# Joining small groups of matmuls in a fused attention and SwiGLU kernel: key products behind a batch's last totals, the turning of values and sums in front of the first query products

One Trainium2 chip (trn2), one core. The metric is the time of one execution on the device in microseconds (us); lower is better.

## The reference

```python
# q, k, v: (4, 4, 1088, 32) fp32; S1, S2: (8, 32)
def phi(x):                                   # features: 8 x 8 products of two sketches
    a = np.einsum('rd,bhsd->bhsr', S1, x)
    b = np.einsum('rd,bhsd->bhsr', S2, x)
    return np.einsum('bhsi,bhsj->bhsij', a, b).reshape(*x.shape[:-1], 64)
q_p, k_p = phi(q), phi(k)
kv = np.einsum('bhsf,bhsd->bhfd', k_p, v)     # "values"
z = np.sum(k_p, axis=2)                       # "sums"
num = np.einsum('bhsf,bhfd->bhsd', q_p, kv)   # "totals": numerator ...
den = np.einsum('bhsf,bhf->bhs', q_p, z)[..., None] + 1e-06    # ... and denominator
attn = num / den
x = attn.transpose(0, 2, 1, 3).reshape(4352, 128)
# feed-forward: w_gate, w_val (128, 1536), w_out (1536, 128)
g = x @ w_gate
out = (g / (1 + np.exp(-g)) * (x @ w_val)) @ w_out
```

## The kernel before

Each of the four batches is three blocks of up to 384 rows of x; a block has 12 "units" (a gate and a value matmul, silu on ScalarE, a product on VectorE that gives `hj`) and 12 down products, which accumulate in one PSUM bank, `acc`. After a block's last down product, VectorE transposes `acc` into the output tile ("store transpose"). The attention of batch b + 1 is a generator, stepped between the units of batch b. The parts that the change touches:

```python
def attention(b):
    for c0, c1 in kpieces:                 # two pieces: 5 and 4 chunks of keys
        turn_k(c0, c1)                     # DVE transpose of the loaded keys
        if c1 == NC and b + 1 < B:
            load_k(b + 1)
        yield
    phk = ...
    prods = [key_products(wide(t)[:, 0, :], *c) for t, c in zip("ab", kpieces)]
    key_features(phk, prods[0], *kpieces[0])
    yield
    key_features(phk, prods[1], *kpieces[1])
    zs = feature_sums(phk)                 # GpSimd
    yield
    kvp = wide("a")
    key_values(kvp[:, 0, :], phk, 0, NC)
    ...                                    # sums, copy to kvs, load_v, turn_q
    yield
    kzp = wide("b")[:, 0, 0 : 2 * P]...
    for t in range(2):
        turn_kv(kvs[:, t, :], kzp[:, t, :])     # "turning" of values and sums
    nc.scalar.copy(kvz[:], kzp)
    yield
    tags = "ab"
    for i, (x0, n) in enumerate(steps):
        phq = query_features(n, query_products(x0, n, tags))
        ...                                # turn_q of the next step, or load_q
        yield
        divide(b, x0, n, totals(n, phq, kvz, side_by_side(tags[0])))
        tags = tags[::-1]
        yield

def down():
    i, j = todo.pop(0)
    if j == 0:
        acc[i] = bank("g0" if i == 1 else "acc")
    nc.tensor.matmul(acc[i][:, 0:n], wo[:, j, :], hidden[i, j][:, 0:n], ...)
    if j == NCH - 1:
        store(i, n)                        # DVE transpose of acc, then DMAs

# (cut) end of the first batch:
while todo:
    for _ in range(3):
        if todo: down()
    next(att, None)
groups = (0, 1, 3, 4, 8, 11, 14, 17, 20, 23, 26, 29)    # units behind which attention steps
for b in range(1, B):
    att = attention(b + 1) if b + 1 < B else None
    for z in range(3 * NCH):
        unit(...)
        for _ in range(2):
            if len(todo) > LAG: down()     # LAG = 2
        if att and z in groups: next(att)
```

`wide("a")` and `wide("b")` are pairs of PSUM banks. The gate and value banks rotate over three banks once the down products have begun.

## Time and profile before

| | before |
|---|---|
| time, median (runs) | 322.25 us (322.06 to 322.41) |
| span of the profiled run | 319.9 us |
| TensorE (PE) busy | 312.2 us, 98% |
| VectorE (DVE), ScalarE (ACT), GpSimd (POOL) busy | 49%, 31%, 12% |
| first key product of the attention passes starts | 59.44 us |
| from there to the start of the last matmul: "the stream" | 256.07 us |

A row of the timeline is its start, its length, the engine, the line and the tiles; an fp32 matmul is two rows. Lengths overlap on PE, so the differences between starts are what is read.

### The profile page before, as it was taken

How to read it: one execution, taken by the hardware profiler on the slowest of the kernel's cores; microseconds unless marked ns; L12 is line 12 of the kernel's file. 1: busy time of each engine (PE TensorE's matmuls, PEld its weight loads, DVE VectorE, ACT ScalarE, POOL GpSimd, SP SyncE). 2: the span in 40 equal slices, each digit the busy share in tenths (PEclk: the TensorE clock that was granted, in tenths of full speed). 3: DMA queues.
4: the chain of work that ended last, by engine and by line, in shares of the span. 5: the costliest groups of instructions: out<-in, count | busy, mean ns of one | idle time of the engine just before them, and what ended most of it. 6: DMA issues, size and time to landing. Idle time of an engine off the chain costs nothing.

```text
span 319.9 us, 5604 instructions
## 1 busy us (share of the span) xinstructions
PE 312.2 (98%) x2300; PEld 193.7 (61%) x2300; DVE 157.8 (49%) x332; ACT 99.0 (31%) x227; POOL 37.6 (12%) x53
## 2 busy tenths in 40 slices
PE   8989999999999999999999999999999999999994
PEld 6545565655556665555666656555667655676664
DVE  4887999442556532554643542354544332323321
ACT  3467755321211322222322222313222222222230
POOL 2324234072000230000000060000000000000000
PEclk9999999999999999999999999999999999999999
DMA  7553490204041201100210100100010100100101
GB/s 206 155 151 100 162 243 2 72 0 97 2 94 27 65 22 50 27 0 2 39 58 0 22 2 0 24 4 2 0 27 0 21 0 2 26 0 0 21 2 25
DMA packets 24665, 13.99 MB, mean 44 GB/s; under 512 B 18368, under 2 KB 22720, under 8 KB 24640
## 3 DMA queue, kind: packets, MB, share of 16 engines
q1 hardware_dynamic: 24000, 13.54, 16.7%
q8 instruction: 18, 0.29, 0.4%
q10 hardware_dynamic: 640, 0.10, 0.2%
q14 instruction: 7, 0.06, 0.1%
HBM read 11.41 MB, written 2.23 MB: 43 GB/s over the span
## 4 chain that ended last, share of the span: by engine, by line
PE 88%; DVE 7%; issue 2%; ACT 1%; POOL 0%; DVEq 0%
PE bank L519 49%; PE bank L547 27%; DVE hj L533 2%; PE a L351 2%; PE a L401 2%; PE b L351 1%; PE bank L197 1%; PE a L307 1%; DVE exp L227 1%; PE a L561 1%; DVE man L231 1%; PE b L401 1%; PE a L276 1%; DVE exp L219 1%; ACT exp L224 1%
## 5 line engine op out<-in xcount | busy, mean ns | idle before, releaser
L533 DVE TENSOR_TENSOR hj<-sg,bank 128x384 f32<-128x384 f32 (+1 forms) x138 | 72.7, 528 | 118.2 <-PE bank L519 117.3
L525 ACT ACTIVATE sg<-bank 128x384 f32<-128x384 f32 (+1 forms) x144 | 67.9, 472 | 162.7 <-PE bank L519 161.9
L519 PE MATMUL bank<-xT,wg 128*128 128x384 f32 (+1 forms) x288 | 113.7, 477 | 1.2 <-POOL wg L235 1.1
L519 PE MATMUL bank<-xT,wv 128*128 128x384 f32 (+1 forms) x288 | 111.5, 469 | 0.5 <-DVE hj L533 0.5
L547 PE MATMUL bank<-hj,wo 128*128 128x384 f32 (+2 forms) x288 | 106.8, 462 | 0.3 <-DVE hj L533 0.2
L519 PEld LDWEIGHTS bank<-xT,wv 128*128 128x128 f32 x288 | 54.4, 190 | 34.5 <-DVE hj L533 2.1
L547 PEld LDWEIGHTS bank<-hj,wo 128*128 128x128 f32 x288 | 53.9, 190 | 33.2 <-issue 2.4
L519 PEld LDWEIGHTS bank<-xT,wg 128*128 128x128 f32 x288 | 52.7, 190 | 32.3 <-issue 3.9
L453 POOL TENSOR_TENSOR zs<-phk 128x1024 f32<-128x1024 f32 x3 | 7.0, 2348 | 115.5 <-PE bank L519 106.0
L379 DVE TENSOR_TENSOR phq<-a,qb 128x384 f32<-128x384 f32 (+1 forms) x11 | 5.8, 531 | 10.7 <-ACT qb L365 10.7
L365 ACT COPY qb<-a 128x384 f32<-128x384 f32 (+1 forms) x11 | 5.1, 460 | 15.1 <-PE b L351 8.6
L351 PE MATMUL a<-qT,sq 32*64 32x192 f32 (+1 forms) x176 | 9.2, 324 | 0.0
L351 PE MATMUL b<-qT,sq 32*64 32x192 f32 (+1 forms) x176 | 9.2, 324 | 0.0
L227 DVE SCALAR_TENSOR_TENSOR exp<-raw,exp 128x384 int32<-128x384 int32 (+2 forms) x14 | 8.6, 618 | 0.9 <-ACT exp L224 0.9
L224 ACT ACTIVATE exp<-exp,rebias 128x384 int32<-128x384 int32 (+3 forms) x15 | 8.2, 550 | 2.7 <-DVE exp L219 2.0
L422 DVE STREAM_TRANSPOSE dT<-a 128x384 f32<-128x384 f32 (+1 forms) x8 | 4.4, 550 | 7.8 <-PE a L401 7.8
L365 ACT COPY qb<-b 128x384 f32<-128x384 f32 (+1 forms) x11 | 5.1, 463 | 9.7 <-PE b L351 6.4
L575 DVE STREAM_TRANSPOSE o<-bank 128x384 f32<-128x384 f32 (+2 forms) x12 | 6.6, 549 | 2.7 <-PE bank L547 2.3
L351 PEld LDWEIGHTS a<-qT,sq 32*64 32x64 f32 x176 | 5.5, 131 | 3.9 <-issue 3.0
L379 DVE TENSOR_TENSOR phq<-b,qb 128x384 f32<-128x384 f32 (+1 forms) x11 | 5.8, 527 | 4.2 <-ACT qb L365 4.2
L231 DVE SCALAR_TENSOR_TENSOR man<-raw,man 128x384 f32<-128x384 uint32 (+2 forms) x14 | 6.9, 493 | 0.0
L225 ACT ACTIVATE man<-man 128x384 f32<-128x384 int32 (+3 forms) x15 | 6.7, 450 | 0.5 <-DVE man L220 0.5
(96 smaller groups left out, 168.9 us busy)
## 6 DMA issues: line engine op xcount, KB each, us to landing
kld<-in_k_dram SPq DMA_DIRECT2D x4, 544.0 KB, 4.1
vld<-in_v_dram SPq DMA_DIRECT2D x12, 144.0 KB, 4.3
qld<-in_q_dram SPq DMA_DIRECT2D x3, 544.0 KB, 3.9
raw<-in_moe_w_out_dram SPq DMA_DIRECT2D x4, 384.0 KB, 5.8
out_dram<-o SPq DMA_DIRECT2D x28, 48.0 KB, 1.9
raw<-in_moe_w_gate_dram SPq DMA_DIRECT2D x3, 384.0 KB, 3.3
raw<-in_moe_w_val_dram SPq DMA_DIRECT2D x3, 384.0 KB, 3.5
out_dram<-o SPq DMA_DIRECT2D x16, 40.0 KB, 1.7
```

The lines of the kernel that those rows point to most:

```text
L224: nc.scalar.activation(e[:], e[:], AF.Relu, bias=rebias[: shape[0], :], scale=8.0)
L227: nc.vector.scalar_tensor_tensor(out=e[:], in0=hi, scalar=-(1 << 31), in1=e[:], op0=ALU.bitwise_and, op1=ALU.bitwise_or,)
L231: nc.vector.scalar_tensor_tensor(out=f, in0=lo, scalar=2.0**-52, in1=f, op0=ALU.mult, op1=ALU.add)
L351: nc.tensor.matmul(parts[g][F * half : F * half + F, t, 0:w], sq[r, t, :, :].rearrange("p i j -> p (i j)"), qT[r, x0 : x0 + n, half, :], s ...
L365: nc.scalar.copy(qb[:, :, 0:w], both[:, :, 1, 0:w])
L379: nc.vector.tensor_tensor(out=phq[:, 2 * pr : 2 * pr + 2, 0:w], in0=both[:, :, 0, 0:w], in1=qb[:, :, 0:w], op=ALU.mult,)
L401: nc.tensor.matmul(halves(nd[t])[half][32 * h : 32 * h + 32, 0:w], kvz[t][r, 32 * h : 32 * h + 32], phq[r, h, 0:w], start=True, stop=True,)
L453: add = lambda o, a, b: nc.gpsimd.tensor_tensor(out=o, in0=a, in1=b, op=ALU.add)
L519: nc.tensor.matmul(o[:, 0:n], w[:, j, :], xT[:, t0 : t0 + n], start=True, stop=True)
L525: nc.scalar.activation(sg[:, 0:n], g[:, 0:n], AF.Silu)
L533: nc.vector.tensor_tensor(out=hj[:, 0:n], in0=sg[:, 0:n], in1=u[:, 0:n], op=ALU.mult)
L547: nc.tensor.matmul(acc[i][:, 0:n], wo[:, j, :], hidden[i, j][:, 0:n], start=(j == 0), stop=(j == NCH - 1),)
```

## The change

Its intent: fewer separate groups of small matmuls in the stream of large ones. The turning and the first query products become one step; the next batch's key products go directly behind the last totals, and their copies behind both of their parts. The key transposes therefore move ahead, and with fewer steps the units at which they stand move too. The diff, with three hunks cut (they split `key_products` into the products and `key_copy`, and call the two one after the other in the start-up):

```diff
@@ -457,15 +459,23 @@
         add(s[:, 0, :], s[:, 0, :], rows[:, 8, :])
         return s[:, 0, :].rearrange("p (h f) -> p h f", h=H)
 
-    def attention(b):
-
-        for c0, c1 in kpieces:
-            turn_k(c0, c1)
-            if c1 == NC and b + 1 < B:
-                load_k(b + 1)
-            yield
+    def next_keys(tag):
+
+        both = wide(tag)
+        for i, c in enumerate(kpieces):
+            key_products(both[:, i, :], *c)
+        return [key_copy(both[:, i, :], *c) for i, c in enumerate(kpieces)]
+
+    def attention(b, prods=None):
+
+
+        if prods is None:
+            for c in kpieces:
+                turn_k(*c)
+                yield
+            load_k(b + 1)
+            prods = next_keys("b")
         phk = apool.tile([P, NC, H, R, R], FP32, tag="phk", name="phk")
-        prods = [key_products(wide(t)[:, 0, :], *c) for t, c in zip("ab", kpieces)]
         key_features(phk, prods[0], *kpieces[0])
         yield
         key_features(phk, prods[1], *kpieces[1])
@@ -484,12 +494,11 @@
         turn_q(*steps[0])
         yield
         kvz = apool.tile([P, 2, P], FP32, tag="kvz", name="kvz", bufs=2)
-        kzp = wide("b")[:, 0, 0 : 2 * P].rearrange("p (t n) -> p t n", t=2)
+        kzp = bank()[:, 0 : 2 * P].rearrange("p (t n) -> p t n", t=2)
         for t in range(2):
             turn_kv(kvs[:, t, :], kzp[:, t, :])
         nc.scalar.copy(kvz[:], kzp)
         kvz = kvz[:, 0, :], kvz[:, 1, :]
-        yield
         tags = "ab"
         for i, (x0, n) in enumerate(steps):
             phq = query_features(n, query_products(x0, n, tags))
@@ -497,9 +506,20 @@
                 turn_q(*steps[i + 1])
             elif b + 1 < B:
                 load_q(b + 1)
+                turn_k(*kpieces[1])
+                if b + 2 < B:
+                    load_k(b + 2)
             yield
-            divide(b, x0, n, totals(n, phq, kvz, side_by_side(tags[0])))
+            nd = totals(n, phq, kvz, side_by_side(tags[0]))
+            last = i + 1 == len(steps)
+            if last and b + 1 < B:
+                prods = next_keys(tags[1])
+            divide(b, x0, n, nd)
+            if i == 1 and b + 1 < B:
+                turn_k(*kpieces[0])
             tags = tags[::-1]
+            if last:
+                return prods
             yield
 
 
@@ -736,28 +757,40 @@
         if z in groups:
             next(att)
     todo.sort()
+    keys = None
+
+    def attend():
+
+        nonlocal att, keys
+        try:
+            if att:
+                next(att)
+        except StopIteration as end:
+            att, keys = None, end.value
+
     while todo:
         for _ in range(3):
             if todo:
                 down()
-        next(att, None)
-    run(att)
-
-
-
-    groups = (0, 1, 3, 4, 8, 11, 14, 17, 20, 23, 26, 29)
+        attend()
+    while att:
+        attend()
+
+
+
+    groups = (0, 1, 6, 9, 12, 15, 18, 21, 24)
     for b in range(1, B):
-        att = attention(b + 1) if b + 1 < B else None
+        att = attention(b + 1, keys) if b + 1 < B else None
         for z in range(3 * NCH):
             i, j = z // NCH, z % NCH
             unit(3 * b + ((0, 2, 1)[i] if b == B - 1 else i), j)
             for _ in range(2):
                 if len(todo) > LAG:
                     down()
-            if att and z in groups:
-                next(att)
-        if att:
-            run(att)
+            if z in groups:
+                attend()
+        while att:
+            attend()
     ps = wide("a")[:, 0, 0:D]
     for j in range(NCH):
         if todo and j % 4 == 0:
```

More of the change, by code (lines that the diff above doesn't have):

```diff
@@ L269, in turn_q, with key_products @@
         )
-    def key_products(ps, c0, c1, aside=False):
+    def key_products(ps, c0, c1):
         for c in range(c0, c1):
@@ L282, in key_products, with key_copy @@
                 )
+    def key_copy(ps, c0, c1, aside=False):
         n = c1 - c0
@@ L620 @@
         turn_k(*c)
-    prods = [
-        key_products(bank(t), *c, aside=(c[1] == NC))
-        for t, c in zip(("g1", "g2", "acc"), fpieces)
-    ]
+    prods = []
+    for t, c in zip(("g1", "g2", "acc"), fpieces):
+        ps = bank(t)
+        key_products(ps, *c)
+        prods.append(key_copy(ps, *c, aside=(c[1] == NC)))
     phk = apool.tile([P, NC, H, R, R], FP32, tag="phk", name="phk")
```

## The prediction

> **What bounds the kernel now.** I read the page's busy table and its row of the granted clock, then the chain that ended last, then the waits by pair, and then the PE timeline around every group of small attention matmuls.
>
> ```profile
> PE 312.2 (98%) x2300; PEld 193.7 (61%) x2300; DVE 157.8 (49%) x332; ACT 99.0 (31%) x227; POOL 37.6 (12%) x53
> ...
> PEclk9999999999999999999999999999999999999999
> ...
> PE 88%; DVE 7%; issue 2%; ACT 1%; POOL 0%; DVEq 0%
> PE bank L519 49%; PE bank L547 27%; DVE hj L533 2%; PE a L351 2%; PE a L401 2%; PE b L351 1%; PE bank L197 1%; PE a L307 1%; DVE exp L227 1%; PE a L561 1%; DVE man L231 1%; PE b L401 1%; PE a L276 1%; DVE exp L219 1%; ACT exp L224 1%
> ```
>
> TensorE is busy in 98% of the span at a full clock and makes up 88% of the chain: a change pays only if it shortens the PE stream, or fills a hole in it. 76% of the chain is the feed-forward matmuls (L519 gate and value, L547 down), which the change does not touch. Busy does not mean free of overhead, because a matmul's row covers its latency as well, so I went by start times. A 384-column fp32 matmul is two rows; in the timeline such pairs start 0.645 us apart, a 320-column pair 0.54 us. Now the key products of the second batch, and the values and sums being turned:
>
> ```profile
> 104.60 0.81 PE L547 MATMUL bank<-hj,wo 128*128 128x384 f32 x2
> 105.34 0.80 PE L276 MATMUL a<-s,kT 128*64 128x64 f32 x20
> 105.97 0.64 PE L276 MATMUL b<-s,kT 128*64 128x64 f32 x16
> 106.54 0.91 PE L519 MATMUL bank<-xT,wg 128*128 128x384 f32 x2
> 107.28 0.81 PE L519 MATMUL bank<-xT,wv 128*128 128x384 f32 x2
> ...
> 122.93 0.81 PE L547 MATMUL bank<-hj,wo 128*128 128x384 f32 x2
> 123.67 0.66 PE L330 MATMUL b<-ident,kvs 128*64 128x128 f32 x8
> 124.25 0.91 PE L519 MATMUL bank<-xT,wg 128*128 128x384 f32 x2
> 125.00 0.81 PE L519 MATMUL bank<-xT,wv 128*128 128x384 f32 x2
> ```
>
> Each group costs something going in and coming out. The pair at 104.60 would have been followed at 105.245 (104.60 + 0.645); the group starts at 105.34, 0.093 late (the unrounded start is 105.338). The first pair behind it takes 107.28 - 106.54 = 0.74 until the next in place of 0.645: its second row starts 0.104 late (0.427 after the first in place of 0.323, at single matmuls). The turning shows the same two figures, and so does every group from 59 us on: 0.093 in, 0.104 out. Between a group's last matmul and the first large one there is a third cost, 0.15 us behind 64 columns, 0.20 behind 128, 0.226 behind 160 and 0.25 behind 192. I count it apart, because it need not go away.
>
> **What the Trainium skill says.** "TensorEngine Tiling (Array Packing)", Key Properties, says that changing the tiling mode, not just the tile, drains the engine. The trace agrees: the small groups are in four modes (128x64, 128x32, 64x32, 32x64), and each change from or to them shows the 0.15 to 0.25 us above. "TensorE: Matmul & The Clock Gate", Part 3, What overlaps and what doesn't, says that a weight load runs beside matmuls in flight only where the row groups differ. That would explain why the first rows on either side of a change are late; the trace shows the lateness, not its cause. "Perfetto Trace Analysis", Identifying the Most-Contended Engine, warns that matmul busy share is a poor measure of room left; I follow it by using start spacing.
>
> **The change, part by part.** Before, an attention batch visits PE nine times: key products; key values with sums; turning; then query products and totals three times over. After, the turning stands directly in front of the first query products (with a rotating bank instead of pair b), and the next batch's key products stand directly behind the last totals, in the two banks of pair b. The instruction order of the built kernel confirms this: no large matmul stands between them, and counts and shapes are otherwise the same. Turning joins in three batches, key products in two (the first attention pass of the loop still has its own): five joins.
>
> What does one join save? Inside a joined group there is still one change of mode. The start-up has such changes from small to small tiles:
>
> ```profile
> 12.31 0.44 PE L330 MATMUL bank<-ident,kvs 128*64 128x128 f32 x4 [0.15 <-DVE kvs L659]
> 12.68 0.56 PE L401 MATMUL a<-phq,kvz 64*32 64x192 f32 x16
> 13.11 0.56 PE L401 MATMUL bank<-phq,kvz 64*32 64x192 f32 x16
> 13.60 0.55 PE L351 MATMUL b<-qT,sq 32*64 32x192 f32 x8
> ```
>
> Stepped down to single matmuls, the last turning matmul there is followed 0.202 us later by the first totals, against 0.203 to a large matmul at 124.25; the last totals by the first query products after 0.253, against 0.252 to a large one. So small to small costs the same drain as small to large, and the drain happens once per group, joined or not. A second row in the new mode is also about 0.05 late inside each group, joined or not. What goes is one entry and one late exit pair: 0.093 + 0.104 = 0.197 us. Five joins: 5 x 0.197 = **0.985 us**. All of it is on PE, which is the path.
>
> The second gain is a side effect at the end of the first batch, where only down products (three per step) fill PE between attention steps. There the query products wait for the divide that frees their banks:
>
> ```profile
> 90.20 1.88 PE L547 MATMUL bank<-hj,wo 128*128 128x320 f32 x6
> 92.01 0.77 PE L351 MATMUL a<-qT,sq 32*64 32x160 f32 x16
> 92.78 0.77 PE L351 MATMUL b<-qT,sq 32*64 32x160 f32 x16
> 93.48 1.88 PE L547 MATMUL bank<-hj,wo 128*128 128x320 f32 x6
> ...
> 92.08 0.56 DVE L447 TENSOR_TENSOR xT<-b,rd 128x384 f32<-128x384 f32 x1
> ```
>
> The b half starts at 92.78, 0.14 after the divide ends at 92.64. The same group without a wait (at 156.5) costs 0.849 us; this one costs 1.563, so 0.71 is waiting. With one step fewer, the gap in front of it holds down products of the block before: two of 384 and one of 320 columns (1.83 us) in place of three of 320 (1.61). The divide ends when it did, counted from the totals, so 0.215 us of useful work moves into the hole: **-0.215 us**. The earlier query products, at 86.1, wait 0.40 and keep three 384-column products in front: no change.
>
> On DVE the key transposes (0.84 and 0.70 us) move: the first behind the second divide, the other behind the last query features. At the end of the first batch DVE then has, after the divide ends (T = 92.64 in the old times): 0.84 transpose, 0.58 store transpose, 2 x 0.49 features, done at T + 2.44. The last totals start at T + 2.66 (95.30): it just fits, with 0.2 us to spare. The second key transpose ends at T + 3.16; the half that reads it starts near T + 4.0. In the second batch's units the divide ends about 2.4 us after its totals and the transpose pushes the next hj to about 3.65; the gate matmul that reuses that bank comes at about 3.97. It fits by 0.3. At the start of the second batch the features (1.49 and 1.21 us) stand between the first three hj; hj of the second unit ends near 102.9, and the bank is next written at 103.3.
>
> Copies: ACT has the same ones, 0.27 to 0.37 us each, off the path. Weights, DMA volume and the whole last batch are unchanged. Sum: 0.985 + 0.215 = 1.20 us, so 322.25 - 1.20 = **321.05 us**.
>
> **Rivals.** (1) *Joined groups drain less*: if pipelining between two small modes hid the drain, each join would save about 0.2 us more, 2.2 in all: 320.05 us. Against it: the start-up changes above cost the full drain. (2) *The join itself saves nothing*: if the in and out costs came from the small tiles and not from the crossing, a joined group would show another 0.1 late start on top of the drain, and only 0.215 is left: 322.0 us. Against it: 0.202 and 0.203 are equal with and without a large matmul behind. (3) *A new DVE wait*: the three margins of 0.2 to 0.4 us above are smaller than they look if DVE instructions spread; one or two missed by 0.3 us give 321.4 to 321.7. For it: DVE time bunches where it was spread; against it: DVE is only 49% busy and its spacing repeats to hundredths in the trace. (4) *Banks*: the rotating bank taken by the turning shifts the rotation of three; a unit could then wait for a value bank that is read later. I counted uses: the next reuse is two units on, behind a finished read. I give this little.
>
> **Range and chances.** The sum of rows is firm, as they repeat to 0.001 us; what is uncertain is the hidden waits (up to +0.7) and the drain (down to -1.0, less likely). With runs that spread 0.35 us, 320.4 to 321.8 should hold eight times in ten. 2% is 6.4 us, five times the effect: within 2% at 0.98.
>
> **What would show it.** Right: five joined groups with no large matmul inside; 0.20 from the last turning matmul to the first query product; about 0.23 from the last totals to the first key product; query products near 92 waiting some 0.5 and not 0.71; the large matmuls' spacing elsewhere unchanged. Wrong: a drain inside a join far from 0.2, or gate matmuls waiting for hj in the second batch behind a divide or a feature product, or last totals at the end of the first batch waiting for DVE. Then the sum fails at the named term.

## More of the kernel before

The stream, taken from starts, is the measure I use most: it leaves out the start-up, which varies from run to run. The prediction shows the key products and the turning before. The last totals of the second attention pass, in the PE timeline:

```profile
162.03 0.70 PE L547 MATMUL bank<-hj,wo 128*128 128x320 f32 x2
162.66 0.77 PE L401 MATMUL a<-phq,kvz 64*32 64x160 f32 x32
163.37 0.81 PE L519 MATMUL bank<-xT,wg 128*128 128x320 f32 x2
164.01 0.70 PE L519 MATMUL bank<-xT,wv 128*128 128x320 f32 x2
```

From 162.03 to 164.01 are 1.98 us, of which two 320-column pairs take 1.08: the group costs 0.90 us. And a store transpose with the two matmuls that follow it, in the timeline of all engines:

```profile
128.43 0.58 DVE L575 STREAM_TRANSPOSE o<-bank 128x384 f32<-128x384 f32 x1
...
128.87 0.81 PE L519 MATMUL bank<-xT,wv 128*128 128x384 f32 x2
...
129.52 0.81 PE L547 MATMUL bank<-hj,wo 128*128 128x384 f32 x2
```

The transpose ends at 129.01; the down product that writes the same bank anew comes at 129.52. Half a microsecond lies between them.

## The result

| | before | after |
|---|---|---|
| time, median, same rounds | 322.15 us (4 runs) | 321.76 us (4 runs) |
| span of the profiled run | 319.9 us | 320.2 us |
| first key product of the attention passes | 59.44 us | 60.08 us |
| stream from there to the last matmul | 256.07 us | 255.67 us |

The ratio is 0.9986, interval 0.9969 to 1.0003: within 2%. (A ratio is the mean time of one kernel's fast runs over that of the other's of the same rounds, so not quite the ratio of the medians quoted.) The time lies in the predicted range, but the gain is a third of the 1.20 us forecast, and the profiled run is even longer. The page of the kernel after, busy row and chain:

```profile
PE 311.3 (97%) x2300; PEld 193.8 (61%) x2300; DVE 156.5 (49%) x332; ACT 98.6 (31%) x227; POOL 37.7 (12%) x53
...
PE 87%; DVE 8%; issue 2%; ACT 1%; POOL 0%; DVEq 0%
```

These shares are of no help at this size; the starts of all matmuls in both traces are. The profiled run after is 0.64 us behind when its first key product starts; up to there the two kernels still have the same instructions in the same program order on each engine. Its first value products had waited for the load of v (11.02 us against 10.34). From there on it gains 0.40 us. First, the joins. The last totals and the next key products after, in the timeline:

```profile
153.79 0.81 PE L567 MATMUL bank<-hj,wo 128*128 128x384 f32 x2
...
154.53 0.77 PE L403 MATMUL a<-phq,kvz 64*32 64x160 f32 x32
...
155.23 1.27 PE L275 MATMUL b<-s,kT 128*64 128x64 f32 x36
...
156.43 0.81 PE L539 MATMUL bank<-xT,wg 128*128 128x320 f32 x2
157.08 0.70 PE L539 MATMUL bank<-xT,wv 128*128 128x320 f32 x2
```

From 153.79 to 157.08 are 3.29 us; less a 384-column and a 320-column pair (0.645 + 0.54) it is 2.10. Apart, the two groups cost 0.90 and 1.39 (the latter in the prediction), 2.29 in all. From unrounded starts each of the two joins of this kind saves 0.198 and each of the three joins with the turning 0.197. The query products that wait for a divide, near 92 us in the prediction's lines, now stand here:

```profile
90.84 0.77 PE L353 MATMUL a<-qT,sq 32*64 32x160 f32 x16
91.39 0.77 PE L353 MATMUL b<-qT,sq 32*64 32x160 f32 x16
92.09 1.07 PE L567 MATMUL bank<-hj,wo 128*128 128x320 f32 x3
```

With their entry of 0.093 they cost 1.347 in place of 1.563. So the whole forecast gain of 1.20 us is there. Of the rest the waits tell; this row of the waits by pair, from 58 us to the end, has no counterpart in the kernel before:

```profile
PEld bank L567 <- DVE o L595: 1.7, 3, 0.6
```

Three times a down product waited for a store transpose. (That is the idle time of the weight-load row; what PE loses is less, and is read from starts.) The first of them, in the timeline:

```profile
128.26 0.58 DVE L424 STREAM_TRANSPOSE dT<-a 128x384 f32<-128x384 f32 x1 [0.90 <-PE a L403]
...
129.96 0.56 DVE L449 TENSOR_TENSOR xT<-a,rd 128x384 f32<-128x384 f32 x1
...
130.44 0.55 DVE L553 TENSOR_TENSOR hj<-sg,bank 128x384 f32<-128x384 f32 x1
130.77 0.81 PE L539 MATMUL bank<-xT,wv 128*128 128x384 f32 x2
130.90 0.57 DVE L595 STREAM_TRANSPOSE o<-bank 128x384 f32<-128x384 f32 x1
...
131.53 0.91 PE L567 MATMUL bank<-hj,wo 128*128 128x384 f32 x2
132.28 0.81 PE L539 MATMUL bank<-xT,wg 128*128 128x384 f32 x2
```

The first totals of a pass now stand behind unit 12, so their divide (from 128.26 to 130.52) lies on VectorE just ahead of the store transpose that belongs behind unit 13. The transpose ends at 131.47, not in time for the down product due at 131.415 (130.77 + 0.645). It starts at 131.53, 0.115 late, and its own second row is another 0.104 late (132.28 - 131.53 = 0.75 for a pair). The same happens at 206.8 us, and behind the last totals at unit 24 in the last pass, at 233.67 us, with 0.266 and 0.105. In the second pass the last totals have key products behind them, which give VectorE another 1.2 us, and there is no wait; in "before, moved onto the store" below, where none stand there, that place waits too. The three sum to 0.219 + 0.217 + 0.371 = 0.807 us. 1.20 - 0.81 = 0.39, against 0.40 measured.

### The profile page after: what moved, and what is told of

The parts are those of the page before. It is cut to its first block, busy times and chain, and to the rows that moved or that the text cites. A ratio compares the mean times of both kernels' runs of the same rounds, so it can differ in the third digit from the quotient of the medians.

```text
span 320.2 us, 5609 instructions
## 1 busy us (share of the span) xinstructions
PE 311.3 (97%) x2300; PEld 193.8 (61%) x2300; DVE 156.5 (49%) x332; ACT 98.6 (31%) x227; POOL 37.7 (12%) x53
## 4 chain that ended last, share of the span: by engine, by line
PE 87%; DVE 8%; issue 2%; ACT 1%; POOL 0%; DVEq 0%
PE bank L539 48%; PE bank L567 27%; DVE hj L553 2%; PE a L403 2%; PE a L353 2%; PE bank L197 1%; PE b L353 1%; PE b L275 1%; PE a L309 1%; DVE exp L227 1%; PE a L581 1%; DVE man L231 1%; PE b L403 1%; PE bank L332 1%; DVE exp L219 1%
## 5 line engine op out<-in xcount | busy, mean ns | idle before, releaser
L298 DVE TENSOR_TENSOR phk<-ka,b 128x1280 f32<-128x1280 f32 (+1 forms) x6 | 8.1, 1342 | 1.7 <-ACT ka L292 1.7
```

The source lines that it names most:

```text
L298: engine.tensor_tensor(out=phk[:, c0:c1, :, :, :].rearrange("p c h i j -> p (c h) i j"), in0=ka.unsqueeze(3).to_broadcast([P, n, R, R]), i ...
```

## The experiments

My theory: joins and the filled hole give 1.20 us, the new position of the totals against the stores takes 0.81 back, and the start-up is chance. Rivals: the change itself slows the start-up; the waits come from the join or the rotating bank; a join saves nothing, or more than an entry and an exit. Seven kernels ran, the first four on one chip, the other three on another; all gave the right result.

| run | stream, us | against before | time, median | ratio to before (interval) |
|---|---|---|---|---|
| before | 256.07 | | 321.83 and 321.97 in the two jobs | |
| the change, again | 255.68 | -0.39 | 321.76 | 1.0001 (0.9989 to 1.0013) |
| two units moved | 254.87 | -1.20 | 320.61 | 0.9967 (0.9955 to 0.9979) |
| turning only | 255.48 | -0.59 | 321.70 | 0.9996 (0.9983 to 1.0009) |
| keys only | 255.84 | -0.23 | 321.76 | 1.0001 (0.9989 to 1.0013) |
| before, moved onto the store | 257.25 | +1.18 | 323.10 | 1.0035 (1.0022 to 1.0049) |
| totals split | 258.76 | +2.69 | 324.47 | 1.0076 (1.0060 to 1.0091) |
| two units moved, holes filled | 254.12 | -1.95 | 320.01 | 0.9937 (0.9925 to 0.9950) |

**The change, again.** No edit.

> The changed kernel itself, once more, to narrow its interval and to see the start-up vary. My account: from the first key products (near 59 us) to the last matmul the PE stream is 0.40 us shorter than before (five joins and one filled hole, -1.20; three new waits of down products for a store transpose, +0.81), in every run alike; the profiled run lost 0.64 us before that to a value load that landed late, which is chance. So the time should be 0.2 to 0.6 us under before, ratio 0.998 to 0.9995. Rival, the change itself slows the start-up: then the start-up is again about 0.6 us late in this profile and in those of the edits of the changed kernel.

The stream is -0.39, as in the first profile. The ratio came out as 1.0001, above the range I gave, because the start-up varies more than the effect: the spans of this kernel's five runs go from 319.7 to 320.9 us, those of the 11 runs of the kernel before from 319.9 to 320.8. The first key product started at 59.44 (before), 60.08 and 59.87 (after), and from 59.40 to 60.79 in the profiles of the six edits. The latest, 60.79, and the earliest, 59.40, both belong to edits of the changed kernel. So a start-up slowed by half a microsecond every time isn't supported. A smaller bias is not ruled out: the six profiles of the changed kernel and its edits have their first key product at 59.88 on average, the three of the kernel before and its edits at 59.52. That the start-up is chance is therefore not shown, only that it varies.

**Two units moved.** The first totals one unit earlier, the last one too:

```diff
-    groups = (0, 1, 6, 9, 12, 15, 18, 21, 24)
+    groups = (0, 1, 6, 9, 11, 15, 18, 21, 23)
```

> The changed kernel with the first totals at unit 11 in place of 12 and the last at 23 in place of 24. If the three new waits are down products waiting for a store transpose that stands behind a divide on VectorE, they vanish: PE stream behind the start-up 0.81 us shorter than the changed kernel's and 1.20 shorter than before's, time near 320.9, ratio near 0.9963. Rival, the rotation of three banks (the turning takes one) or the DVE load as such makes the waits: they stay at other places, and the time stays near the changed kernel's, ratio 0.9985.

All three waits are gone, and the stream is 1.20 us shorter than before's, to the hundredth. The rotating bank, still in use, makes no wait. The same place in the timeline of this kernel:

```profile
129.87 0.58 DVE L595 STREAM_TRANSPOSE o<-bank 128x384 f32<-128x384 f32 x1
...
130.96 0.81 PE L567 MATMUL bank<-hj,wo 128*128 128x384 f32 x2
```

The store transpose ends at 130.45, half a microsecond ahead of the down product, as in the kernel before.

**Turning only**, on the kernel before:

```diff
-        kzp = wide("b")[:, 0, 0 : 2 * P].rearrange(...)
+        kzp = bank()[:, 0 : 2 * P].rearrange(...)
 ...
-        yield                                   # behind the turning
-    groups = (17, 19, 21, 23, 27, 29)           # first batch
+    groups = (17, 19, 21, 23, 27)
-    groups = (0, 1, 3, 4, 8, 11, 14, 17, 20, 23, 26, 29)
+    groups = (0, 1, 3, 4, 8, 14, 17, 20, 23, 26, 29)
```

> The kernel before with only the turning joined to the first query products (rotating bank, no step between); all other steps at the units where before has them, query products of the first pass at their old place. Three joins: if a join saves one entry (0.093) and one late exit pair (0.104), the PE stream is 3 x 0.197 = 0.59 us shorter and no new wait appears; ratio 0.998. If joining saves nothing, 0.0 and 1.000; if it also saved a drain, 1.2.

The stream is 0.59 us shorter: three joins at 0.197. It settles what one join is worth. The timed ratio alone could not have told 0.59 from nothing.

**Keys only**: the changed kernel with the turning apart in pair b again, and the units of before:

```diff
-        kzp = bank()[:, 0 : 2 * P].rearrange(...)
+        kzp = wide("b")[:, 0, 0 : 2 * P].rearrange(...)
 ...
+        yield                                   # behind the turning
-    groups = (0, 1, 6, 9, 12, 15, 18, 21, 24)
+    groups = (3, 4, 8, 11, 14, 17, 20, 23, 26, 29)
```

> The changed kernel with the turning apart again (pair b, its own step) and every other step at the unit where the kernel before has it, so that only the next key products behind the last totals are left of the change. Two joins: 2 x 0.197 = 0.39 us shorter PE stream, no store wait (totals stand at 17, 23 and 29 as before), ratio 0.9988. Rival, the moved key transposes make DVE late for the query features or the next gate bank: a new wait of 0.2 us or more behind the second divide or at the next batch's first units.

Half a miss. Both joins save 0.198 (groups of 1.996 us), but the stream is shorter by 0.23 and not by 0.39. The rival's wait is there, once:

```profile
153.72 0.83 DVE L260 STREAM_TRANSPOSE kT<-kld 128x640 f32<-128x640 f32 x1
...
154.48 0.85 DVE L554 TENSOR_TENSOR hj<-sg,bank 128x320 f32<-128x320 f32 x2
154.98 0.30 PEld L540 LDWEIGHTS bank<-xT,wg 128*128 128x128 f32 x2 [0.52 <-DVE hj L554]
```

The key transpose behind the second divide makes `hj` late, and a gate matmul waits 0.064 for its bank, with 0.104 on its second row: 0.17. The second totals stand behind unit 23 here, so that the units behind them have 320 columns and take less time than the 384-column ones behind unit 18, where the change has them and PE loses nothing.

**Before, moved onto the store**: no join, only the units.

```diff
-    groups = (0, 1, 3, 4, 8, 11, 14, 17, 20, 23, 26, 29)
+    groups = (0, 1, 3, 4, 8, 9, 10, 12, 15, 18, 21, 24)
```

> The kernel before with no join, only its steps moved so that the first totals stand at unit 12 and the last at 24, as in the changed kernel. If the position alone makes the store wait: 0.219 us at each first totals and 0.371 at each last totals, in two batches, +1.18 us in all, ratio 1.0037. If the waits come from the join or from the rotating bank: none, 1.000.

+1.18 us, from four waits (0.117, 0.263, 0.114 and 0.266, each with 0.104 to 0.105 on the second row: 1.18). The weight load of the down product at 131.73 names the store:

```profile
131.10 0.58 DVE L575 STREAM_TRANSPOSE o<-bank 128x384 f32<-128x384 f32 x1
...
131.73 0.30 PEld L547 LDWEIGHTS bank<-hj,wo 128*128 128x128 f32 x2 [0.57 <-DVE o L575]
```

"Two units moved" takes the waits away from the change; this run gives them to a kernel without it. So the position of the attention steps is enough to make them, and the joins and the rotating bank are not needed.

**Totals split**: one down product in the middle of each of nine totals groups of the changed kernel.

```diff
         for t in (1, 0):
+            if t == 0 and between:
+                between()
 ...
-            nd = totals(n, phq, kvz, side_by_side(tags[0]))
+            nd = totals(n, phq, kvz, side_by_side(tags[0]), down)
```

> The changed kernel with one down product moved into the middle of each of its nine totals groups of the attention passes, so that each group crosses between large and small tiles once more; the same matmuls otherwise. A crossing should add an entry 0.093, a drain in place of an ordinary step (0.252 - 0.115 = 0.137), a late pair 0.104 and perhaps 0.025 of a late second row: 0.36 each, 3.2 us in all, time near 325. If the lateness belongs to the small tiles and not to the crossing: near 0. The divide starts later too, so up to 0.5 more may come from it.

The stream is 3.09 us longer than that of the changed kernel. The totals at 129 us, in the PE timeline:

```profile
128.55 0.81 PE L569 MATMUL bank<-hj,wo 128*128 128x384 f32 x2
129.28 0.56 PE L405 MATMUL a<-phq,kvz 64*32 64x192 f32 x16
129.77 0.91 PE L569 MATMUL bank<-hj,wo 128*128 128x384 f32 x2
130.61 0.56 PE L405 MATMUL a<-phq,kvz 64*32 64x192 f32 x16
131.10 0.91 PE L541 MATMUL bank<-xT,wg 128*128 128x384 f32 x2
```

Both halves start 0.09 late, both have the drain to the large matmul behind them, and both large pairs are late. From unrounded starts the two halves cost 1.366 us with their late pairs, the whole group 1.008: 0.358 for one more crossing, nine times 3.22. The rest fits too. The three store waits are gone here (-0.81), one gate matmul waits for `hj` at 148.81 (+0.45), and the query products that had been helped wait longer again (+0.22): 3.08. So the lateness belongs to the crossing between tilings and not to the small tiles as such.

The kept traces say more of what a crossing costs than the prediction has. At every change of tiling the next matmul starts behind the last one by that one's columns, at 0.84 ns each (0.323 us for 384), and 0.09 to 0.10 us more: 0.416 behind 384 columns, 0.252 behind 192, 0.203 behind 128, 0.152 behind 64. So by these figures the entry's 0.093 and the drain behind a group are one cost, met at each change of tiling; a joined group has three such changes where two groups apart have four. The late second row goes with the weight load. A large row's load as a rule starts 0.27 or 0.32 us ahead of it, beside the row before. From 58 us on, the rows whose load started at most 0.003 us ahead were followed 0.10 us late, 27 of 27 before and 25 of 25 after: all groups, and the three down products that had waited for a store. With more than 0.1 us of lead none was, except where the next row itself waited. Why a load stays back at a change of tiling, no run shows.

**Two units moved, holes filled.** The better version: the second edit, and four down products in place of three ahead of the two query groups that wait for a divide.

```diff
+    fill = iter((3, 4, 3, 4))
     while todo:
-        for _ in range(3):
+        for _ in range(next(fill, 3)):
```

> The two moved units of the second run, and at the end of the first batch four down products in place of three ahead of the two query groups that wait for a divide. Three down products of 384 leave 0.40 us of wait, the mixed three leave 0.50; a fourth is 0.645 and 0.54: both waits go, -0.90. With -1.20: PE stream 2.1 us shorter than before's, time near 320.0, ratio 0.9935. If the totals then wait for the features in turn, part of the 0.90 comes back there.

The stream is 1.95 us shorter than before's, the time 320.01 us, ratio 0.9937: clear of noise, though under 2%. It did not run in one job with the changed kernel, but its stream is 1.55 us shorter than that one's (255.67), and its slowest run (320.11) is under the changed kernel's fastest (321.49). Of the 0.90 us forecast for the holes 0.75 came. Each of the two query groups still costs 0.075 us more than an unhindered one (1.030 against 0.955, and 0.923 against 0.849); what holds them I have not followed.

## Why the prediction was right, and where it fell short

- *PE is the path, and start spacing is its measure*: right. Every number that later fitted came from starts; the busy share moved by a point and told nothing.
- *A join saves one entry and one late exit pair, 0.197, and the drain stays*: right in size. Three joins gave 0.59, both kinds of join save 0.197 to 0.198 in the trace. Rival 1 (less drain) and rival 2 (nothing) fall. That the entry is a cost apart from the drain does not hold (see "Totals split"), nor does the explanation of the lateness by row groups (last section).
- *Five joins, 0.985*: right, all five are in the trace.
- *The query products near 92 us wait 0.5 and not 0.71, 0.215 gained*: right, 1.347 against 1.563, a difference of 0.216.
- *The margins on VectorE*: this step failed. The prediction checked the features, the key transposes and the next `hj`, and each of those held, with no wait on PE. One of them had nothing to spare: in the second pass of the changed kernel the gate's weight load at 145.66 us waited for the `hj` behind the key transpose, 0.026 us longer than the idle time before such a load elsewhere (0.158 against 0.132). The 0.3 us of slack had been counted to the gate matmul; the load stands 0.3 us ahead of it. The prediction left out the store transpose, whose bank the next block's down product reuses two units later. The term was put at zero; it measured +0.81 us. Rival 3 had the kind of wait right (VectorE work bunched) and put it at 0.35 to 0.65 us, but named other waits. Its own wait, `hj` behind the moved key transpose, costs PE time only in "keys only", where the units behind are narrower, and in "totals split" (a gate matmul, 0.45 us).
- *Rival 4, the rotating bank*: no wait from it in any run.
- *The size*: 1.20 forecast, 0.40 in the stream, and in the two timed comparisons 0.4 us and nothing. The range held because it left 0.75 us for hidden waits, and with luck: 321.76 is 0.04 us inside its edge, and from the 322.25 us that the prediction started with, the 0.40 us of the stream would have given 321.85, outside it. Without the store waits the change is worth what was forecast: "two units moved" is 1.22 us under before by the medians of its job (320.61 against 321.83).

The Trainium skill's statement that a change of tiling mode drains the engine ("TensorEngine Tiling (Array Packing)", Key Properties) agrees with the splitting experiment, which gives a size: 0.36 us for one more crossing, of which about 0.14 is the drain in place of an ordinary step.

## What to carry to other kernels

Count crossings between large and small matmul tilings on a full TensorE and join those that can stand together; each costs a fixed sum that busy shares don't show. When a step moves, list everything that stands behind it on every in-order engine, the housekeeping too (here the store transpose), and ask which bank each frees and when it is needed next. Where the start-up varies more than the effect, compare the stretch behind it between starts in the traces: in the two profiles of the changed kernel it repeated to 0.01 us, where its times spread by 1 us.

## What the Trainium skill lacked or had wrong

- "TensorEngine Tiling (Array Packing)", Key Properties, says that a change of mode drains, without a figure: 0.15 us behind a 64-column fp32 matmul to 0.25 behind a 192-column one, from its start to that of the first matmul in the next mode, the same whether that one is large or small. Behind a large one it is 0.363 for 320 columns and 0.416 for 384.
- No page gives the other cost: a large fp32 matmul whose weight load could not start ahead of it has its second row 0.104 us late, after a change of mode and after a wait for a bank alike (27 of 27 rows before, 25 of 25 after).
- "TensorE: Matmul & The Clock Gate", Part 3, What overlaps and what doesn't, which the prediction cites, lets weight loads run beside matmuls only where the row groups differ. Here the loads of full-array rows do so too: before the change, the load at 128.551 us starts 0.002 behind a full-array row, takes 0.19, and the next row starts 0.323 behind the first. The measurement decides.
